# Zeroing the experts' output buffer on another engine, and decoding 64-bit weights in wider pieces of single tasks

## The chip, the core and the metric

The kernel runs on one core of a Trainium2 chip. The metric is the device time of one execution in microseconds (us); lower is better. The kernel before was timed in three runs: 807.14, 810.14 and 810.48 us, median 810.14.

## The reference: what is computed

Three stages follow one another.

1. Causal attention with a decay: 4 batches, 8 heads, 576 positions, head size 64. The result, laid out as 2304 tokens of 512 numbers, is the input `x` of the second stage.
2. A mixture of 8 experts in which every token goes to one expert, that of the largest logit: `h = max(x[mask] @ w1[e], 0)`, `out[mask] = gate * (h @ w2[e])`, with `w1` of 512 x 1024 and `w2` of 1024 x 512 per expert.
3. A shared block on all tokens: `h = max(x @ w1, x @ w2, x @ w3)` and `h @ w_out`, with three matrices of 512 x 768 and one of 768 x 512. In the reference, `1.0 / np.sqrt(d_model)` makes these four matrices float64, and the products of them run in float64.

## The kernel before, in words

Attention takes the first part, and then the function `moe` does the two other stages. All matrix products there use a split of each number into a rounded part and a remainder ("hi" and "lo"): three matmuls (lines 906 to 908, function `mm3`) stand for one product. Every tile that goes into such a product must first be rounded (a copy, line 934) and then have its remainder taken (a subtraction: line 951 for expert weights, line 1022 for shared weights, line 1069 for tokens, line 1123 for the hidden layer, line 1181 for the shared block's input).

**Order.** The engines run their instructions in the order in which the program issues them. That order is not written by hand: the class `Sched` plans it when the kernel is built. Every task names an engine (or a choice of two), a planned cost in us, a due time (`prio`), the tasks that it waits for and a buffer that it takes or gives back. `run` takes, step by step, the task that could start first by the planned times, and among equals the one due first. Within `moe`, `sd.bias` makes VectorE (1.0) dearer than GpSimd (0.3) where a task may run on either. What an engine really does later deviates from the planned times, but the order stays.

**Experts.** The 8 experts are taken in order of size, with fixed capacities `CAP` of 384 down to 256 tokens. For each, tokens are gathered from memory by GpSimd (`gather`, line 1051), transposed on TensorE into one of two PSUM buffers (`flip`, line 1058), rounded and split (lines 934 and 1069, the latter always on VectorE). Expert weights come in quarters of 128 x 1024 through three staging tiles `stg` and a ring of four split quarters. The first expert's quarters 1 to 3 are loaded from ScalarE's queue, the others from SP's. The results go into `Y`, four tiles of 128 x 2512, the experts one behind the other, each at an offset read at run time. `Y` is set to zero first by four GpSimd memsets (`zero`, line 1088).

**Shared weights.** The four float64 matrices lie in memory as pairs of 32-bit words, 12 keys of 128 x 1024 values. `shared_piece` (line 988) loads them and rebuilds float32 numbers from the two words (`bits`, line 977): five VectorE instructions shift and mask the high word into sign, exponent and mantissa (lines 982, 984), add the top three bits of the low word (985), and set numbers too small to zero by a comparison of the magnitude (983, 986). This is the decoding. It is done for 256 values at a time, as one planned task of 1.35 us, and writes to a tile `decv` of its own; rounding and remainder follow. The first 8 keys (`M2EARLY`) are prepared during the expert stage and stay; their loads of 128 x 512 words share one buffer `std`, given back at the end of the decoding. The last 4 keys come at the end through `stg` and the ring.

**The shared block** takes 6 chunks of 384 tokens. Matmuls into `pm` are followed by the maximum over the three matrices on VectorE (line 1222, tile `tm`), the split of the hidden layer `g` (lines 934 and 1233), the last product `po` (lines 1248 to 1250) and a scatter to memory.

Of the kernel before, what the change touches and what calls it, by code (L numbers as in the profile page):

```python
# [6 lines left out]
F32 = mybir.dt.float32  # L7
# [31 lines left out]
RING = 4  # L39
# [80 lines left out]


class Sched:
    """Orders the instructions of all engines: at each step the task that could start first, then the most urgent."""

    HOP = 0.2

# [784 lines left out]
def moe(tc, g, x_dram, w1, w2, m2, mo, out, rp, es):  # L911
# [11 lines left out]
    KC, FC, F2C, m2c, nchunk = DM // 128, FF // 128, F2 // 128, MC // 128, N // MC  # L923
    Y = [yp.tile([128, YW], F32, name=f"Y{d}") for d in range(KC)]

    sd = Sched({"o": 2, "stg": 3, "std": 1, "ring": RING, "scr": 3, "decv": 2, "y": 6}, 0.0)
    sd.bias = {"DVE": 1.0, "Pool": 0.3}
    act = lambda n: 0.06 + n / 1200
    dve = lambda n: 0.15 + n / 960
# [47 lines left out]
    def bits(raw, q, v, n):  # L977
        r = raw.rearrange("p (n w) -> p n w", w=2)[:, 256 * q:256 * q + 256]
        lo, hi = r[:, :, 0], r[:, :, 1]
        t = scr.tile([128, 256], I32, tag="dect", name=f"dt{n}", bufs=1)  # L980
        u = scr.tile([128, 256], I32, tag="decu", name=f"du{n}", bufs=1)
        nc.vector.tensor_scalar(out=t, in0=hi, scalar1=3, scalar2=0x3FFFFFF8, op0=ALU.logical_shift_left, op1=ALU.bitwise_and)  # L982
        nc.vector.tensor_scalar(out=u, in0=hi, scalar1=0x7FFFFFFF, scalar2=None, op0=ALU.bitwise_and)
        nc.vector.scalar_tensor_tensor(out=t, in0=hi, scalar=-0x40000000, in1=t, op0=ALU.bitwise_and, op1=ALU.bitwise_or)
        nc.vector.scalar_tensor_tensor(out=t, in0=lo, scalar=29, in1=t, op0=ALU.logical_shift_right, op1=ALU.bitwise_or)  # L985
        nc.vector.scalar_tensor_tensor(out=v, in0=u, scalar=float(897 << 20), in1=t.bitcast(F32), op0=ALU.is_ge, op1=ALU.mult)

    def shared_piece(key, early, use):
        w, j = key
        src = (mo[j] if w == "o" else m2[w, j]).bitcast(I32)  # L990
        nq = 1 if early else 2
        size = 512 * nq
        lows = []
        for h in range(2048 // size):
            raw = {}

            def load(e, h=h, raw=raw):
                if early:
                    t = raw[0] = std.tile([128, size], I32, tag="std", name=f"sd_{w}_{j}_{h}")
                else:  # L1000
                    t = raw[0] = stg.tile([128, size], I32, tag="stg", name=f"sd_{w}_{j}_{h}")
                nc.sync.dma_start(out=t, in_=src[:, size * h:size * h + size])

            pool_ = "std" if early else "stg"
            ld = sd.task("SP", 0.75 * nq, load, use - 8, [ahead.get(pool_)], get=(pool_, (key, h)), lat=2.0)
            ahead[pool_] = ld
            for q in range(nq):
                i = h * nq + q
                sl = slice(256 * i, 256 * i + 256)

                def dec(e, q=q, i=i, raw=raw):
                    raw[1 + q] = scr.tile([128, 256], F32, tag="decv", name=f"dv_{w}_{j}_{i}", bufs=2)
                    bits(raw[0], q, raw[1 + q], f"_{w}_{j}_{i}")

                def hi(e, q=q, i=i, raw=raw, sl=sl):
                    if key not in weight:
                        weight[key] = (m2p.tile([128, 2, 1024], F32R, name=f"m_{w}_{j}") if early else
                                       ring.tile([128, 2, 1024], F32R, tag="ring", name=f"m_{w}_{j}"))
                    copy(e, weight[key][:, 0, sl], raw[1 + q])

                def lo(e, q=q, raw=raw, sl=sl):
                    ENG[e].tensor_tensor(out=weight[key][:, 1, sl], in0=raw[1 + q], in1=weight[key][:, 0, sl].bitcast(F32),
                                         op=ALU.subtract)

                td = sd.task("DVE", 1.35, dec, use - 4, [ld], get=("decv", (key, i)),
                             rel=[(pool_, (key, h))] if q == nq - 1 else [])
                new = not early and i == 0
                th = sd.task(("ACT", "DVE"), (act(256), 0.2), hi, use - 3, [td, ahead.get("ring") if new else None],
                             get=("ring", key) if new else None)
                if new:  # L1030
                    ahead["ring"] = th
                lows.append(sd.task(("DVE", "Pool"), (dve(256), 0.69), lo, use - 3, [th], rel=[("decv", (key, i))]))
        wsplit[key] = lows

    def xtiles(name):
        return [xp.tile([128, KC, PADW], F32R, tag=f"x{i}", name=f"x{i}_{name}") for i in range(2)]
# [48 lines left out]
        else:  # L1085
            expert_piece(1, 0, q, now + 3.8 * q, [first], "ACT")
    xdone = {0: tokens(0, now, [])}
    zero = [sd.task("Pool", 2.1, lambda e, d=d: nc.gpsimd.memset(Y[d], 0.0), now + 16) for d in range(KC)]
    mkeys = [(w, j) for j in range(3) for w in range(3)] + [("o", j) for j in range(3)]
    total = now + sum(CAP) * 192 / 2400  # L1090
    for i, key in enumerate(mkeys[:M2EARLY]):
        shared_piece(key, True, now + 30 + (total - now - 34) * (i + 1) / M2EARLY)
    yprev, yall = [[] for _ in range(4)], []
    ydone = []
    hlast, yev_last = [], []
    for k in range(E):
# [43 lines left out]
        for i, (q, d) in enumerate(order):  # L1140
            def ymm(e, q=q, d=d, k=k, C=C):
                if q == 0:
                    hh["y", k, d] = ps_y.tile([128, 512], F32, tag="y", name=f"py{k}_{d}")
                py = hh["y", k, d]
                w = weight[2, k, q].rearrange("p s (f d) -> p s f d", f=2)
                for f in range(2):
                    fc = 2 * q + f
                    ds_ = slice(128 * d, 128 * d + 128)
                    mm3(nc, py[:, 0:C], w[:, 0, f, ds_], w[:, 1, f, ds_], hh[k, fc][:, 0, 0:C], hh[k, fc][:, 1, 0:C],
                        fc == 0, fc == FC - 1)  # L1150

            end = not any(q2 == q for q2, _ in order[i + 1:])
            last[d] = sd.task("PE", 6 * C / 2400, ymm, now, [wsplit[2, k, q], h_lo[2 * q], h_lo[2 * q + 1], last.get(d)],
                              get=("y", ("y", k, d)) if q == 0 else None, rel=[("ring", (2, k, q))] if end else [])
            pieces[q].append(last[d])
            now += 6 * C / 2400
            if q == 3:
                def yev(e, d=d, k=k, C=C):
                    o = Y[d][:, bass.ds(reg(ENG[e], "offi", k, YW - C), C)] if k else Y[d][:, 0:C]
                    copy(e, o, hh["y", k, d][:, 0:C])  # L1160

                prev = [ydone[-1][d]] if ydone else [zero[d]]
                t = sd.task(("ACT", "DVE"), (act(C), dve(C)), yev, now, [last[d]] + prev + [sorted_], rel=[("y", ("y", k, d))])
                yev_last.append(t)
        ydone.append(yev_last[-KC:])
# [1 line left out]
        yall = [last[d] for d in range(KC)]  # L1167
        hlast = h_pe
    for i, key in enumerate(mkeys[M2EARLY:]):
        shared_piece(key, False, now + 24 + 4 * i)  # L1170

    def ysplit(c, use, before):
        done = []
# [268 lines left out]
```

## Time and profile before

| what | value |
|---|---|
| median of three runs | 810.14 us (807.14 to 810.48) |
| span of the profiled execution, first to last instruction | 808.7 us |
| TensorE busy with matmuls | 744.5 us, 92% of the span |
| VectorE | 485.8 us, 60% |
| ScalarE | 364.8 us, 45% |
| GpSimd | 267.9 us, 33% |
| mean DMA rate | 112 GB/s |

The page gives no other time of the profiled execution than its span; the median of the runs lies 1.4 us (0.2%) above it. The busy share of TensorE is an average over stages with different limits, and a matmul that is counted as busy isn't always at its peak, because its end is modelled. What counts is when a stage starts, where TensorE stands still in it, which engine let it go on, and at which clock it then runs (PEclk, as a share of full speed). A row of the timeline has the start, the duration, the engine, the line of the program, the instruction, the written and read tiles with their shapes and how many instructions were merged; in brackets stand the idle time before it and what ended it. A name such as `dt` or `x` is the program's tile name, buffer numbers left out.

### The profile page before, as it was taken

The numbers are of one execution on the slowest core, as the hardware profiler recorded it, in microseconds if no ns is written. First come the engines' busy times: TensorE is split into PE (matmuls) and PEld (weight loads), VectorE is DVE, ScalarE is ACT, GpSimd is POOL, SyncE is SP. The second block draws the span as 40 slices with busy tenths as digits, with TensorE's granted clock in tenths as the row PEclk, the third lists the DMA queues.
The fourth block names the chain that finished last, engine by engine and source line by source line (L and its number), as shares of the span: only waits on it lengthen the run. The fifth ranks groups of instructions, "written<-read, shape, count | busy, mean of one in ns | idle before, by whom it ended". The sixth has DMA issues, their size and how long they took to land.

```text
span 808.7 us, 13612 instructions
## 1 busy us (share of the span) xinstructions
PE 744.5 (92%) x4862; PEld 685.5 (85%) x4862; DVE 485.8 (60%) x1197; ACT 364.8 (45%) x892; POOL 267.9 (33%) x214
## 2 busy tenths in 40 slices
PE   2989999999929899998998999979999999999996
PEld 1768878778719899998998999969989999899995
DVE  6888888887487997888777857981111211212110
ACT  5768878978626344553453544231121211212111
POOL 7465352540062543434344202341121211212111
PEclk9999999999959999999998999999999999999999
DMA  9958785831146556666476554300000000000001
GB/s 220 239 138 203 178 191 137 201 78 30 32 121 216 148 172 202 187 198 197 145 208 189 168 180 132 104 1 39 1 40 1 6 34 1 40 1 14 27 1 41
DMA packets 46919, 90.20 MB, mean 112 GB/s; under 512 B 23576, under 2 KB 23576, under 8 KB 46848
## 3 DMA queue, kind: packets, MB, share of 16 engines
q1 hardware_dynamic: 43264, 77.83, 35.1%
q0 software_dynamic: 3152, 9.88, 3.5%
q10 hardware_dynamic: 432, 1.57, 0.5%
q8 instruction: 40, 0.66, 0.3%
q14 instruction: 31, 0.25, 0.1%
HBM read 74.97 MB, written 9.44 MB: 104 GB/s over the span
## 4 chain that ended last, share of the span: by engine, by line
PE 61%; DVE 20%; DMA 13%; issue 3%; ACT 2%; POOL 0%; SPq 0%; DVEq 0%; POOLq 0%; ACTq 0%
PE pm L907 8%; PE pm L908 8%; PE pm L906 8%; DMA sd<-in_m_dram 7%; PE s L344 7%; PE po L459 6%; PE t L397 4%; DMA stg<-in_w_dram 3%; PE po L1250 2%; PE po L1249 2%; PE po L1248 2%; PE pb L478 2%; DVE dt L982 2%; DVE w L951 2%; DVE dt L985 2%
## 5 line engine op out<-in xcount | busy, mean ns | idle before, releaser
L1222 DVE TENSOR_TENSOR tm<-pm,tm 128x384 f32<-128x384 f32 x72 | 40.1, 557 | 199.1 <-PE pm L908 197.9
L906 PE MATMUL pm<-x_y,m 128*128 128x384 f32 x432 | 144.7, 335 | 3.3 <-DVE tm L1222 3.3
L907 PE MATMUL pm<-x_y,m 128*128 128x384 f32 x432 | 144.6, 335 | 0.0
L908 PE MATMUL pm<-x_y,m 128*128 128x384 f32 x432 | 144.4, 334 | 0.0
L381 ACT ACTIVATE P<-P,nm 128x576 f32<-128x576 f32 (+4 forms) x160 | 88.3, 554 | 18.2 <-DVE nm L361 17.6
L344 PE MATMUL s<-R,At 128*128 128x192 f32 (+1 forms) x192 | 70.8, 378 | 16.5 <-DVE At L271 11.1
L906 PEld LDWEIGHTS pm<-x_y,m 128*128 128x128 f32 x432 | 81.1, 188 | 4.5 <-DVE tm L1222 4.3
L1233 POOL TENSOR_TENSOR g<-tm,g 128x384 fp32r<-128x384 f32 x36 | 38.3, 1064 | 138.1 <-ACT g L934 138.0
L907 PE MATMUL ph<-x,w 128*128 128x384 f32 (+7 forms) x256 | 79.7, 311 | 2.8 <-DVE x L1069 2.8
L934 ACT ACTIVATE w<-stg 128x1024 fp32r<-128x1024 f32 x64 | 67.4, 1054 | 32.2 <-DMA stg<-in_w_dram 25.2
L907 PEld LDWEIGHTS pm<-x_y,m 128*128 128x128 f32 x432 | 81.1, 188 | 0.6 <-POOL x_y L1181 0.3
L906 PE MATMUL py<-h,w 128*128 128x384 f32 (+7 forms) x256 | 81.4, 318 | 0.0
L908 PE MATMUL py<-h,w 128*128 128x384 f32 (+7 forms) x256 | 80.0, 313 | 1.2 <-DVE w L951 1.2
L908 PEld LDWEIGHTS pm<-x_y,m 128*128 128x128 f32 x432 | 81.1, 188 | 0.0
L906 PE MATMUL ph<-x,w 128*128 128x384 f32 (+7 forms) x256 | 79.9, 312 | 0.7 <-ACT x L934 0.7
L907 PE MATMUL py<-h,w 128*128 128x384 f32 (+7 forms) x256 | 79.9, 312 | 0.0
L908 PE MATMUL ph<-x,w 128*128 128x384 f32 (+7 forms) x256 | 79.7, 311 | 0.2 <-DVE w L951 0.2
L951 DVE TENSOR_TENSOR w<-stg,w 128x1024 fp32r<-128x1024 f32 x47 | 64.3, 1371 | 21.9 <-ACT w L934 21.9
L361 DVE CUSTOM_DVE_ANT_0 P<-s,mask 128x288 f32<-128x288 f32 (+4 forms) x160 | 64.3, 421 | 10.8 <-PE s L344 6.5
L934 ACT ACTIVATE g<-tm 128x384 fp32r<-128x384 f32 x36 | 18.9, 524 | 110.7 <-DVE tm L1222 110.6
L321 POOL TENSOR_TENSOR At<-q,At 64x1152 fp32r<-64x1152 f32 x15 | 40.3, 2687 | 76.7 <-DVE At L433 24.8
L344 PE MATMUL s<-R,Bt 66*128 66x192 f32 (+1 forms) x192 | 59.6, 317 | 4.1 <-DMA Bt<-At 4.1
(244 smaller groups left out, 1704.5 us busy)
## 6 DMA issues: line engine op xcount, KB each, us to landing
stg<-in_w_dram SPq DMA_DIRECT2D x61, 512.0 KB
q<-in_q_dram SPq DMA_DIRECT2D x32, 288.0 KB
k<-in_k_dram SPq DMA_DIRECT2D x32, 288.0 KB
sd<-in_m_dram SPq DMA_DIRECT2D x32, 256.0 KB
Bt<-At SPq DMA_DIRECT2D x16, 288.0 KB
v<-in_v_dram SPq DMA_DIRECT2D x4, 1024.0 KB
x_dram<-XL SPq DMA_DIRECT2D x64, 64.0 KB
sd_o<-in_mo_dram SPq DMA_DIRECT2D x6, 512.0 KB
```

The costliest lines, as they stand in the source:

```text
L321: nc.gpsimd.tensor_tensor(out=At[i][64:128], in0=raws[p][0][64:128], in1=At[i][64:128].bitcast(F32), op=ALU.subtract)
L344: nc.tensor.matmul(st[:, 0:wp], lt[0:kk, r, ROW0[t]:ROW0[t] + 128], rt[0:kk, r, j0:j0 + wp], start=(ps_i == 0), stop=(ps_i == 1))
L361: nc.vector.tensor_tensor_reduce(out=P[0:n, j0:j0 + w], in0=st_.pop((h, t, k))[0:n, 0:w], in1=g.mask[0:n, m0:m0 + w], scale=-0.125, scalar ...
L381: nc.scalar.activation(out=P[0:n, 0:ext], in_=P[0:n, 0:ext], func=AF.Exp, bias=nm[0:n, k:k + 1], scale=-1.0, accum_out=sums[b][0:n, t, h % ...
L459: nc.tensor.matmul(po[64 * r:64 * r + 64, lo - c0:w], vt[b][0:n, a, (2 * hp + r) * D:(2 * hp + r + 1) * D], PT[(2 * p + r) % NPT][0:n, a, ...
L906: nc.tensor.matmul(out, whi, xhi, start=start, stop=False)
L907: nc.tensor.matmul(out, whi, xlo, start=False, stop=False)
L908: nc.tensor.matmul(out, wlo, xhi, start=False, stop=stop)
L934: nc.scalar.activation(out=out, in_=in_, func=AF.Copy)
L951: ENG[e].tensor_tensor(out=w[:, 1], in0=t, in1=w[:, 0].bitcast(F32), op=ALU.subtract)
L1222: nc.vector.tensor_tensor(out=mx[0], in0=mx["p", w][:, 0:MC], in1=mx[0], op=ALU.max)
L1233: ENG[e].tensor_tensor(out=ht[:, 1, :], in0=mx[0], in1=ht[:, 0, :].bitcast(F32), op=ALU.subtract)
```

## The change

The planner's cost for a piece, the buffers and the tasks change, not the arithmetic.

- `Y` is zeroed by ScalarE (`clear`): four copies of a broadcast column times 0, of the columns from 384 to 2304 alone, planned at 1.8 us each, behind the first expert's last weight quarter (`wsplit[1, 0, 3]`). Only the results of the second and later experts wait for it.
- `bits` isn't called any more. A piece is 512 values (128 x 1024 words, for early keys too). The five steps are single planned tasks of 0.4 or 0.65 us, 2.75 in all. The masked high word is put over the high words in the loaded tile (`size`), and the result over its low words (`flush`); a scratch tile `dec` of 512 columns, a single one, holds the rest. So the loaded tile is given back only behind the remainder (`lo`).
- The loads of the early keys wait for the split of `wsplit[1, 0, 3]` or of the key before the previous one.

```
-    sd = Sched({"o": 2, "stg": 3, "std": 1, "ring": RING, "scr": 3, "decv": 2, "y": 6}, 0.0)
+    sd = Sched({"o": 2, "stg": 3, "std": 1, "ring": RING, "scr": 3, "dec": 1, "y": 6}, 0.0)
...
-    def shared_piece(key, early, use):
+    def shared_piece(key, early, use, deps):
...
+        for h in range(2):
...
+                t = (std if early else stg).tile([128, 1024], I32, tag=pool_, name=f"sd_{w}_{j}_{h}")
+                nc.sync.dma_start(out=t, in_=src[:, 1024 * h:1024 * h + 1024])
+                t = t.rearrange("p (n w) -> p n w", w=2)
+                raw[0], raw[1] = t[:, :, 0], t[:, :, 1]
+
+            def exponent(e, h=h, raw=raw, tmp=tmp):
+                tmp[0] = scr.tile([128, 512], I32, tag="dec", name=f"dec_{w}_{j}_{h}", bufs=1)
+                nc.vector.tensor_scalar(out=tmp[0], in0=raw[1], scalar1=3, scalar2=0x3FFFFFF8, op0=ALU.logical_shift_left,
+                                        op1=ALU.bitwise_and)
+
+            def sign(e, raw=raw, tmp=tmp):
+                nc.vector.scalar_tensor_tensor(out=tmp[0], in0=raw[1], scalar=-0x40000000, in1=tmp[0], op0=ALU.bitwise_and,
+                                               op1=ALU.bitwise_or)
+
+            def last(e, raw=raw, tmp=tmp):
+                nc.vector.scalar_tensor_tensor(out=tmp[0], in0=raw[0], scalar=29, in1=tmp[0], op0=ALU.logical_shift_right,
+                                               op1=ALU.bitwise_or)
+
+            def size(e, raw=raw):
+                nc.vector.tensor_scalar(out=raw[1], in0=raw[1], scalar1=0x7FFFFFFF, scalar2=None, op0=ALU.bitwise_and)
+
+            def flush(e, raw=raw, tmp=tmp):
+                nc.vector.scalar_tensor_tensor(out=raw[0].bitcast(F32), in0=raw[1], scalar=float(897 << 20),
+                                               in1=tmp[0].bitcast(F32), op0=ALU.is_ge, op1=ALU.mult)
...
+            ld = sd.task("SP", 1.5, load, use - 8, deps + [ahead.get(pool_)], get=(pool_, (key, h)), lat=2.0)
...
+            for i, (fn, cost) in enumerate(((exponent, 0.4), (sign, 0.65), (last, 0.65), (size, 0.4), (flush, 0.65))):
+                t = sd.task("DVE", cost, fn, use - 4, [t, ahead.get("dec") if i == 0 else None], get=("dec", (key, h)) if i == 0 else None,
+                            rel=[("dec", (key, h))] if i == 4 else [])
...
+            th = sd.task(("ACT", "DVE"), (act(512), 0.4), hi, use - 3, [t, ahead.get("ring") if new else None],
+                         get=("ring", key) if new else None)
...
+            lows.append(sd.task(("DVE", "Pool"), (dve(512), 1.3), lo, use - 3, [th], rel=[(pool_, (key, h))]))
...
-    zero = [sd.task("Pool", 2.1, lambda e, d=d: nc.gpsimd.memset(Y[d], 0.0), now + 16) for d in range(KC)]
+    def clear(e, d):
+        nc.scalar.activation(out=Y[d][:, CAP[0]:N], in_=g.ident[:, 0:1].to_broadcast([128, N - CAP[0]]), func=AF.Copy, scale=0.0)
+
+    zero = [sd.task("ACT", 1.8, lambda e, d=d: clear(e, d), now + 16, [wsplit[1, 0, 3]]) for d in range(KC)]
...
+    shared = [wsplit[1, 0, 3]]
...
-        shared_piece(key, True, now + 30 + (total - now - 34) * (i + 1) / M2EARLY)
+        shared.append(shared_piece(key, True, now + 30 + (total - now - 34) * (i + 1) / M2EARLY, [shared[max(0, i - 1)]]))
...
-                prev = [ydone[-1][d]] if ydone else [zero[d]]
+                prev = [ydone[-1][d], zero[d]] if ydone else []
```

## Rows read from the trace of the kernel before

**Rows 1.** Busy time by stretch: us, then each engine's busy us, clock, DMA
```profile
core 0 of [0], span 808.7 us
242.50:246.00 3.50, 3.46 (x10) 3.06 (x11) 3.21 (x8) 2.51 (x3) 1.40 (x2) 0.54 0.92 339
242.50:496.20 253.70, 240.39 (x1636) 236.35 (x1637) 200.04 (x373) 123.21 (x215) 87.09 (x56) 0.97 0.59 185
436.90:443.60 6.70, 5.49 (x24) 5.46 (x25) 6.28 (x10) 2.16 (x5) 5.47 (x4) 0.50 0.59 176
496.20:545.00 48.80, 44.15 (x239) 40.97 (x238) 45.19 (x92) 15.33 (x37) 21.91 (x25) 1.00 0.17 55
545.00:797.00 252.00, 252.00 (x1366) 240.70 (x1365) 45.32 (x72) 47.83 (x92) 51.51 (x50) 1.00 0.04 17
```

**Rows 2.** Timeline of all engines, 231 to 243 us
```profile
231.01 0.95 POOL L1051 DMA_INDIRECT gat<-x_dram,gidx  x1 [0.31 <-issue]
...
231.75 8.84 DVE L776 CAST offi<-off 128x8 int32<-128x8 f32 x1
231.95 8.62 POOL L1088 MEMSET Y<- 128x2512 f32 x4
...
234.37 6.23 DVE L1069 TENSOR_TENSOR x<-xt,x 128x512 fp32r<-128x512 f32 x2
...
240.70 1.11 PE L1058 MATMUL xt<-ident,gat 128*128 128x128 f32 x4 [6.01 <-DVE ov L779]
...
241.85 0.60 ACT L934 ACTIVATE x<-xt 128x512 fp32r<-128x512 f32 x1 [6.52 <-PE xt L1058]
...
242.06 0.34 ACTq L964 DMA_DIRECT2D stg<-in_w_dram  x1
...
242.50 0.69 PE L906 MATMUL ph<-x,w 128*128 128x384 f32 x1 [0.69 <-ACT x L934]
```

**Rows 3.** Chain of waits, 228 to 262 us: start, us, what
```profile
228.24 4.31 DMA gat<-x_dram,gidx
```

**Rows 4.** TensorE's waits, expert stage: total us, times, longest; six rows
```profile
PE xt L1058 <- DVE x L1069: 8.9, 6, 3.6
...
PE ctps L859 <- DVE x L1069: 0.2, 1, 0.2
```

**Rows 5.** VectorE's groups by shape, 242 to 545 us: count, busy us, mean ns
```profile
L951 DVE TENSOR_TENSOR w<-stg,w 128x1024 fp32r<-128x1024 f32 x46 | 56.1, 1223 | 21.9 <-ACT w L934 21.9
L982 DVE TENSOR_SCALAR dt<-sd 128x256 int32<-128x256 int32 x36 | 22.3, 619 | 14.3 <-DMA sd<-in_m_dram 13.8
...
L982 DVE TENSOR_SCALAR dt_o<-sd_o 128x256 int32<-128x256 int32 x12 | 3.5, 288 | 0.1
```

**Rows 6.** Timeline: an undisturbed decoding (five rows), and one beside GpSimd
```profile
244.69 0.29 DVE L982 TENSOR_SCALAR dt<-sd 128x256 int32<-128x256 int32 x1
...
246.00 0.43 DVE L986 SCALAR_TENSOR_TENSOR dv<-du,dt 128x256 f32<-128x256 int32 x1
...
505.29 0.83 POOL L1022 TENSOR_TENSOR m<-dv,m 128x256 fp32r<-128x256 f32 x1 [1.34 <-ACT m L934]
...
505.44 0.83 DVE L983 TENSOR_SCALAR du_o<-sd_o 128x256 int32<-128x256 int32 x1
```

**Rows 7.** ScalarE's and GpSimd's groups by shape up to 545 us
```profile
L934 ACT ACTIVATE w<-stg 128x1024 fp32r<-128x1024 f32 x63 | 66.3, 1054 | 26.4 <-DMA stg<-in_w_dram 25.2 <-issue 0.4 <-ACT w L934 0.3
...
L951 POOL TENSOR_TENSOR w<-stg,w 128x1024 fp32r<-128x1024 f32 x17 | 42.2, 2483 | 22.6 <-ACT w L934 22.5
...
L1022 POOL TENSOR_TENSOR m_o<-dv_o,m_o 128x256 fp32r<-128x256 f32 x12 | 9.6, 803 | 20.1 <-ACT m_o L934 20.1
```

**Rows 8.** SP's DMA queue: its waits, 227 to 545 us
```profile
SPq L1002 <- DVE dt L985: 108.3, 32, 14.2
```

**Rows 9.** TensorE's waits, 496.2 to 545 us; three rows
```profile
PE pm L906 <- DVE tm L1222: 3.3, 3, 1.7
...
PE po L1248 <- ACT g L934: 0.6, 1, 0.6
```

More of the change, by code (lines that the diff above doesn't have):

```diff
@@ L986, in bits @@
         nc.vector.scalar_tensor_tensor(out=v, in0=u, scalar=float(897 << 20), in1=t.bitcast(F32), op0=ALU.is_ge, op1=ALU.mult)
-    def shared_piece(key, early, use):
+    def shared_piece(key, early, use, deps):
         w, j = key
         src = (mo[j] if w == "o" else m2[w, j]).bitcast(I32)
-        nq = 1 if early else 2
-        size = 512 * nq
         lows = []
-        for h in range(2048 // size):
-            raw = {}
+        pool_ = "std" if early else "stg"
+        for h in range(2):
+            raw, tmp = {}, {}
+            sl = slice(512 * h, 512 * h + 512)
@@ L997, in load @@
             def load(e, h=h, raw=raw):
[L998 to L1005, printed above, removed]
@@ L1006, in shared_piece @@
-            ahead[pool_] = ld
[L1007 to L1032, printed above, removed]
@@ new lines, in flush, with hi @@
+            def flush(e, raw=raw, tmp=tmp):
+                nc.vector.scalar_tensor_tensor(out=raw[0].bitcast(F32), in0=raw[1], scalar=float(897 << 20),
+                                               in1=tmp[0].bitcast(F32), op0=ALU.is_ge, op1=ALU.mult)
+            def hi(e, raw=raw, sl=sl):
+                if key not in weight:
+                    weight[key] = (m2p.tile([128, 2, 1024], F32R, name=f"m_{w}_{j}") if early else
+                                   ring.tile([128, 2, 1024], F32R, tag="ring", name=f"m_{w}_{j}"))
+                copy(e, weight[key][:, 0, sl], raw[0].bitcast(F32))
@@ new lines, in lo @@
+            def lo(e, raw=raw, sl=sl):
+                ENG[e].tensor_tensor(out=weight[key][:, 1, sl], in0=raw[0].bitcast(F32), in1=weight[key][:, 0, sl].bitcast(F32),
+                                     op=ALU.subtract)
+            ld = sd.task("SP", 1.5, load, use - 8, deps + [ahead.get(pool_)], get=(pool_, (key, h)), lat=2.0)
+            ahead[pool_] = ld
+            t = ld
+            for i, (fn, cost) in enumerate(((exponent, 0.4), (sign, 0.65), (last, 0.65), (size, 0.4), (flush, 0.65))):
+                t = sd.task("DVE", cost, fn, use - 4, [t, ahead.get("dec") if i == 0 else None], get=("dec", (key, h)) if i == 0 else None,
+                            rel=[("dec", (key, h))] if i == 4 else [])
@@ L1033, in shared_piece @@
+            ahead["dec"] = t
+            new = not early and h == 0
+            th = sd.task(("ACT", "DVE"), (act(512), 0.4), hi, use - 3, [t, ahead.get("ring") if new else None],
+                         get=("ring", key) if new else None)
+            if new:
+                ahead["ring"] = th
+            lows.append(sd.task(("DVE", "Pool"), (dve(512), 1.3), lo, use - 3, [th], rel=[(pool_, (key, h))]))
         wsplit[key] = lows
+        return lows[-1]
     def xtiles(name):
@@ L1169, in moe @@
     for i, key in enumerate(mkeys[M2EARLY:]):
-        shared_piece(key, False, now + 24 + 4 * i)
+        shared_piece(key, False, now + 24 + 4 * i, [])
     def ysplit(c, use, before):
```

## The prediction, made before the changed kernel was run

> **What bounds the kernel now.** I read the stages first (busy time by stretch): where TensorE stands idle, and at which clock. Up to 220 us lies attention, which the diff does not touch. Then comes a hole until the first expert matmul at 242.5. The expert stage (242.5 to 496.2) holds 253.7 us, 240.4 of them counted busy, at a mean clock of 0.97; a passage of 48.8 us follows with 44.15 busy; the last chunks (545 to 797) are full [rows 1]. So time can be won in three places alone: the hole in front of the expert stage, the stage's inner gaps, and the passage.
>
> Then the timeline of the start. VectorE's small CAST of the offsets lasts 8.84 us, as GpSimd's four memsets of Y begin 0.2 us behind it and last 8.62 us together; both end at 240.6 [rows 2]. Two token splits of VectorE (6.23 us for two) end there too. The third transposition of tokens waited 6.01 us, then ScalarE's copy came at 241.85 and the first expert matmul at 242.50 [rows 2]. The memsets therefore hold VectorE, and VectorE holds TensorE.
>
> Then TensorE's waits in the expert stage: six groups, 14.0 us, of which 8.9 are transpositions that wait for VectorE's token split, which frees their PSUM buffer [rows 4]. The clock adds to it: 0.97 over 253.7 us is 7.6 us lost, of which 1.6 belong to the first 3.5 us of the stage (0.54); the rest (6.0) lies in later stretches such as 436.9 to 443.6, at 0.50 after a wait of TensorE of up to 3.6 us [rows 1, 4]. Last, what VectorE does: the decoding of the shared weights costs 126.1 us in ten groups, 48 pieces of 2.63 us each [rows 5].
>
> **The change part by part.**
>
> *The zeroing leaves GpSimd.* Without it the CAST is short and the splits follow ScalarE's copies at once. The first gather takes 4.31 us from its issue to the landing; the third is issued at 231.01, so its tokens are there at about 235.4 [rows 2, 3]. The transposition takes 1.1, ScalarE's copy began 1.15 us behind the start of the transposition (240.70 to 241.85) and the first matmul 0.65 behind that [rows 2]: 235.5 + 1.15 + 0.65 = 237.3, or 5.2 us earlier than 242.50. The weights must come along: ScalarE issues the third quarter's load right behind that copy (242.06, [rows 2]), so it moves too; the first quarter's split waited for the memsets like all else. Bounds: 5.2 us is the whole of it; the least is 2.7, if the planner, finding GpSimd free, gives it a weight remainder there (2.48 us, [rows 7]) that holds the CAST. I take 5.2, nearest to the rows of this very stretch.
>
> *ScalarE writes the zeros.* Four copies of 1920 columns; a 1024-column copy takes 1.054 us [rows 7], so at most 1.98 each, 7.9 together. ScalarE works 123 of 253.7 us in the stage [rows 1], and only the second expert's results need the zeros, which now depend on the first expert's last weight quarter. Queued behind a clear are ReLUs and weight roundings; six PSUM buffers cover the ReLUs, three staging tiles the roundings. If that cover is gone, one clear (2.0 us) shows; below that nothing. I take 0.7.
>
> *The decoding in pieces of 512.* An undisturbed piece of 256 takes from 244.69 to 246.43, 1.74 us [rows 6]. Two-input instructions cost 0.43 at 256 columns and 1.22 at 1024 [rows 5, 6], 1.03 ns per column above a fixed 0.17; at 512 each of the three adds 0.26, and the two one-input steps half of that (0.29 at 256, [rows 6]): 1.74 + 0.79 + 0.26 = 2.8, against 3.48 for two of 256. 24 pieces save 16 us of VectorE. The in-place steps write with a stride of two words; if the one-input form lost its rate there, 24 times 0.27 = 6.5 us come off. [...] The rows show 0.17 us per instruction, and the measurement decides.
>
> The pieces are also disturbed: 126.1 - 48 x 1.74 = 42.6 us of the decoding is waiting. A one-input step of 0.29 takes 0.83 while GpSimd does a remainder of 0.83 [rows 6]. Remainders of 512 on GpSimd should take 1.35 (0.80 at 256, 2.48 at 1024, [rows 7]); if each held VectorE for all its length, 24 x (2.8 + 1.35) = 100, a saving of 26 us; if the waits halve with the instructions, 67 + 21 = 88, a saving of 38. [...] I take 26, some 17 in the expert stage and 9 in the passage.
>
> *Single tasks.* One decoding stood in the plan as 1.35 us and could not be parted; it takes 2.63. Now 2.75 is planned per piece and 4.1 expected, and a token split can go between two steps. VectorE so falls behind its plan by 1.4 us per 512 columns instead of 2.6. VectorE worked 200 of 253.7 us in the expert stage [rows 1], so it does not bound the stage as a whole: what it decides is the moments when the split of tokens is late. I take half of the 14.0 us of waits and half of the 6.0 us of clock: 10 us. Bounds: 0 (the waits only move) and 18 (all but the last weights).
>
> *One buffer of 1024 words, held to the remainder.* SP waited 108.3 us, 32 times, for the early buffer [rows 8], with the experts' weight loads queued behind. Now it is 16 pieces, and the buffer is held for rounding and remainder too. A cycle: load about 4.5 (estimate, from the gather's 4.31, [rows 3]), decoding 4.1, rounding 0.6 (1.054 at 1024, [rows 7]), remainder 1.35, handing over 0.5: 11 us. 16 cycles are 176 us. The loads now wait for the first expert's last quarter, whose load follows the one at 242.06 [rows 2] that moves to 237: they begin near 250 and the pieces end near 426, some 55 us ahead of their use in the passage. I cost it at nothing; at 14.5 us per cycle this cover is gone.
>
> *The passage.* VectorE is busy 45.2 of 48.8 us there, and TensorE waits 4.6 us, 3.3 of them for VectorE's maximum that frees PSUM [rows 1, 9]. With the 9 us less decoding I take 4.0 of the 4.6; bounds 0 and 4.6. Behind it TensorE is full, so nothing is late next.
>
> **The sum.** 5.2 - 0.7 + 10 + 4.0 = 18.5 us. The profiled span is 808.7 [rows 1]; with 18.5 off it is 790.2, and the median of the runs (810.14) lies 1.4 above that span: 791.6, rounded up to 792.
>
> **The rivals.**
> *Only the start is won.* GpSimd's remainders and weight remainders (17 of 2.48 us, [rows 7]) still hold VectorE, the planner finds another order, and as many splits of tokens come late. For it: each such weight remainder alone is longer than what is needed to make a split late, and none is removed. Against it: 26 us less VectorE work. 5.2 - 0.7, and 0 to 2 of the passage: about 803 to 806.
> *All waits go.* 5.2 + 18 + 4.6: about 782. For it: the waits are few and all of one kind. [...]
> *Given back.* The start is earlier, but weights come no earlier (SP behind the early buffer), so that TensorE waits later for what it won: 807 to 812. For it: 108.3 us of SP's waits; against it: hardly a wait of TensorE names a weight today.
> *Slower: the single wide buffer.* Load, decoding, rounding and remainder now stand one behind the other with nothing overlapped. Place: SP's queue, with expert loads behind it; it decides from 14.5 us per cycle. At 16.5 the early weights end 16 x 2 = 32 us late; the decoding begun early covers part, and the remainder of the cost, some 15 us, stands ahead of the passage: 810 - 5 + 15 = 820. For it: GpSimd takes 2.48 us for a weight in front of a remainder, and such a delay now holds the buffer. Against it: the 11 us estimated.
>
> **How the numbers follow.** Forecast (785 to 801) 0.56; only the start (801 to 806) 0.19; all waits go (779 to 785) 0.09; given back 0.08; slower 0.08. About 0.5%, 4 us, is what a measurement of this kernel can tell from no change. Faster by more (below 806.1): 0.84; within: 0.08; slower: 0.08. The range 781 to 808 leaves out the slow rival, half of what is given back, and a little below.
>
> **What would show it.** The first expert matmul near 237.3 (over 240: the first step is wrong). The CAST under 0.5 us. Decoding groups near 100 us on VectorE. TensorE's waits for token splits near 7 us, with fewer stretches at half clock. No wait of TensorE for the maximum before 545. If SP's waits for the early buffer grow above 108 us and TensorE's waits name weights, the slow rival holds; if the start is earlier and the expert stage is longer by as much, the gain was given back.

## The result and the profile after

The changed kernel takes 784.12 us (median of 4, 782.49 to 785.84) against 808.64 us for the kernel before, measured with it: ratio 0.970, 95% interval 0.966 to 0.974, or 24.5 us less. The profiled executions differ by 25.4 us (808.7 and 783.3). Measured again beside other versions (the last experiment) the ratio was 0.969 (0.965 to 0.972).

First the stages of the changed kernel, busy time by stretch (columns as in [rows 1]): expert stage, passage, last chunks.

```profile
237.90:477.06 239.16, 234.97 (x1636) 231.28 (x1637) 188.45 (x289) 128.25 (x201) 67.58 (x43) 0.99 0.56 195
477.06:525.80 48.74, 48.74 (x266) 46.31 (x265) 39.91 (x54) 15.13 (x30) 21.23 (x18) 1.00 0.17 60
525.80:771.00 245.20, 245.20 (x1337) 235.05 (x1335) 45.03 (x72) 46.78 (x90) 49.37 (x48) 1.00 0.04 17
```

The expert stage begins at 237.90 and not 242.50, lasts 239.2 us and not 253.7, and runs at 0.99; the passage is full [rows 1]. So the 25.4 us are 4.6 in front of the expert stage (0.2 of them from attention), 14.5 inside it, and 6.3 behind it: 306.2 us from the first matmul of the shared block to the end, against 312.5.

The start in the timeline:

```profile
228.04 1.08 POOL L1065 DMA_INDIRECT gat<-x_dram,gidx  x1 [45.59 <-DVE rr L689]
...
230.82 0.95 POOL L1065 DMA_INDIRECT gat<-x_dram,gidx  x1 [0.30 <-issue]
...
231.57 0.20 DVE L776 CAST offi<-off 128x8 int32<-128x8 f32 x1
...
236.12 1.09 PE L1072 MATMUL xt<-ident,gat 128*128 128x128 f32 x4 [1.85 <-DVE ov L783]
...
237.90 0.69 PE L906 MATMUL ph<-x,w 128*128 128x384 f32 x1 [0.69 <-ACT x L934]
```

The CAST of 8.84 us [rows 2] takes 0.20. Nothing holds VectorE any more, and the third transposition starts 5.3 us after the issue of its gather at 230.82. This trace has no landing for that gather; in the trace of the same kernel measured again it lands 5.5 us after its issue, so I take the transposition to wait for the gather.

TensorE's waits in the expert stage are five rows with 4.7 us together, where there were 14.0 [rows 4]; none is a transposition. In the passage there is none.

```profile
PE ph L907 <- DVE x L1083: 2.1, 2, 1.7
PE py L906 <- DVE h L1141: 0.8, 1, 0.8
PE ph L908 <- DVE w L951: 0.7, 1, 0.7
PE ph L906 <- ACT x L934: 0.7, 1, 0.7
PE py L908 <- DVE w L951: 0.4, 1, 0.4
```

VectorE's groups (columns as in [rows 5]): the decoding is ten groups again, 93.8 us in all instead of 126.1. The costliest group, and one of equal shape that nothing holds up (997 and 689 ns a piece):

```profile
L1009 DVE SCALAR_TENSOR_TENSOR dec<-sd,dec 128x512 int32<-128x512 int32 x18 | 17.9, 997 | 0.6
...
L1013 DVE SCALAR_TENSOR_TENSOR dec<-sd,dec 128x512 int32<-128x512 int32 x18 | 12.4, 689 | 0.4
```

ScalarE's clears stand between ReLUs of the first expert, 1.80 us each, and TensorE waits for nothing from 245 to 270 us:

```profile
249.15 1.80 ACT L1103 ACTIVATE Y<-ident 128x1920 f32<-128x1920 f32 x1
250.85 0.49 ACT L1135 ACTIVATE h<-ph 128x384 fp32r<-128x384 f32 x1
251.23 1.05 ACT L934 ACTIVATE w<-stg 128x1024 fp32r<-128x1024 f32 x1
```

### The profile page after: what moved, and what is told of

The parts are those of the page before. It is cut to its first block, busy times and chain, and to the rows that moved or that the text cites. A ratio compares the mean times of both kernels' runs of the same rounds, so it can differ in the third digit from the quotient of the medians.

```text
span 783.3 us, 13403 instructions
## 1 busy us (share of the span) xinstructions
PE 738.9 (94%) x4862; PEld 682.3 (87%) x4862; DVE 461.9 (59%) x1076; ACT 368.2 (47%) x870; POOL 237.7 (30%) x189
## 4 chain that ended last, share of the span: by engine, by line
PE 75%; DVE 9%; DMA 7%; issue 4%; ACT 1%; POOL 1%; SPq 1%; POOLq 0%; DVEq 0%; ACTq 0%
PE pm L907 10%; PE pm L906 10%; PE pm L908 10%; PE s L344 6%; PE po L459 6%; PE t L397 4%; PE ph L908 3%; PE ph L907 3%; PE py L906 3%; PE py L908 3%; PE ph L906 3%; PE py L907 3%; PE po L1268 3%; PE po L1267 3%; PE po L1266 3%
## 5 line engine op out<-in xcount | busy, mean ns | idle before, releaser
L344 PE MATMUL s<-R,At 128*128 128x192 f32 (+1 forms) x192 | 71.3, 380 | 14.9 <-DVE At L271 10.5
L934 ACT ACTIVATE w<-stg 128x1024 fp32r<-128x1024 f32 x63 | 66.2, 1056 | 33.3 <-DMA stg<-in_w_dram 14.4
L951 DVE TENSOR_TENSOR w<-stg,w 128x1024 fp32r<-128x1024 f32 x54 | 70.2, 1304 | 19.3 <-ACT w L934 18.9
L906 PE MATMUL py<-h,w 128*128 128x384 f32 (+7 forms) x256 | 79.5, 311 | 0.8 <-DVE h L1141 0.8
L1251 POOL TENSOR_TENSOR g<-tm,g 128x384 fp32r<-128x384 f32 x34 | 36.5, 1074 | 141.4 <-ACT g L934 141.4
L908 PE MATMUL py<-h,w 128*128 128x384 f32 (+7 forms) x256 | 78.5, 307 | 0.4 <-DVE w L951 0.4
L907 PE MATMUL py<-h,w 128*128 128x384 f32 (+7 forms) x256 | 78.2, 305 | 0.0
L361 DVE CUSTOM_DVE_ANT_0 P<-s,mask 128x288 f32<-128x288 f32 (+4 forms) x160 | 64.4, 422 | 11.1 <-PE s L344 6.7
```

Of the source, the lines that this page charges most:

```text
L344: nc.tensor.matmul(st[:, 0:wp], lt[0:kk, r, ROW0[t]:ROW0[t] + 128], rt[0:kk, r, j0:j0 + wp], start=(ps_i == 0), stop=(ps_i == 1))
L361: nc.vector.tensor_tensor_reduce(out=P[0:n, j0:j0 + w], in0=st_.pop((h, t, k))[0:n, 0:w], in1=g.mask[0:n, m0:m0 + w], scale=-0.125, scalar ...
L906: nc.tensor.matmul(out, whi, xhi, start=start, stop=False)
L907: nc.tensor.matmul(out, whi, xlo, start=False, stop=False)
L908: nc.tensor.matmul(out, wlo, xhi, start=False, stop=stop)
L934: nc.scalar.activation(out=out, in_=in_, func=AF.Copy)
```

## The experiments

Theory A: three separate gains, at the start from the memsets, in the expert stage and in the passage from the new decoding, the latter two because VectorE has less to do and its work comes in finer steps. The rivals stand with the runs. All ratios are to the kernel before on the same chip, with the 95% interval; the changed kernel stands at 0.969 to 0.970.

**The zeroing alone.**
```
 (kernel before)
-    zero = [sd.task("Pool", 2.1, lambda e, d=d: nc.gpsimd.memset(Y[d], 0.0), now + 16) for d in range(KC)]
+    zero = [sd.task("ACT", 1.8, lambda e, d=d: clear(e, d), now + 16, [wsplit[1, 0, 3]]) for d in range(KC)]
...
-                prev = [ydone[-1][d]] if ydone else [zero[d]]
+                prev = [ydone[-1][d], zero[d]] if ydone else []
```


> The kernel before with the zeroing alone moved to ScalarE, behind the first expert's last weight quarter; the decoding stays in 256-column pieces of one task. Theory A (three separate gains: 4.6 us at the start from the memsets, some 14 in the expert stage from the new decoding, some 6 in the passage from the new decoding): the first expert matmul near 238, expert stage again 250 to 256 us long with token splits late and stretches at half clock, passage with its 4.6 us of waits; in all 3 to 6 us faster than before (about 804). Theory B (the freed VectorE time at the start also sets the expert stage right): 12 us or more faster, under 797.

Measured: 804.09 us, ratio 0.991 (0.988 to 0.994), 7.6 us less. The first matmul came 8.7 us after the first gather instead of 14.3, the expert stage was 252.5 us long with 13.9 us of waits, and the rest 312.4, as before. Theory B falls: the time that VectorE gets back at the start doesn't set the stage right (it is 1.2 us shorter).

**The decoding alone.**
```
 (changed kernel)
-    zero = [sd.task("ACT", 1.8, lambda e, d=d: clear(e, d), now + 16, [wsplit[1, 0, 3]]) for d in range(KC)]
+    zero = [sd.task("Pool", 2.1, lambda e, d=d: nc.gpsimd.memset(Y[d], 0.0), now + 16) for d in range(KC)]
...
-                prev = [ydone[-1][d], zero[d]] if ydone else []
+                prev = [ydone[-1][d]] if ydone else [zero[d]]
```


> The changed kernel with the four GpSimd memsets back at the start, the new decoding kept. Theory A: first expert matmul at 242.5 again with a CAST of over 8 us, expert stage 238 to 243 us long without half clock, passage without waits; 4 to 5 us slower than the changed kernel (about 789). Theory B: the expert stage's waits return, 795 or more.

Measured: 796.7 us, ratio 0.981 (0.978 to 0.984). That is 9 us slower than the changed kernel, not 4 to 5. The hole is back (14.26 us from the first gather to the first matmul, as before), and the expert stage takes 247.2 us, 8 more than in the changed kernel, with 11.1 us of waits. The passage is without a wait. Together the two halves of the change give 7.6 + 15.5 = 23.1 us of the 24.5, so they add up within their intervals. TensorE's waits in the expert stage of this run, three rows of six:

```profile
PE ph L907 <- DVE x L1083: 4.3, 2, 3.2
PE xt L1072 <- DVE x L1083: 2.3, 2, 1.5
...
PE py L908 <- POOL w L951: 1.2, 1, 1.2
```

**The zeroing on GpSimd, planned late.**
```
 (changed kernel, clear)
-        nc.scalar.activation(out=Y[d][:, CAP[0]:N], in_=g.ident[:, 0:1].to_broadcast([128, N - CAP[0]]), func=AF.Copy, scale=0.0)
+        nc.gpsimd.memset(Y[d][:, CAP[0]:N], 0.0)
...
-    zero = [sd.task("ACT", 1.8, ...
+    zero = [sd.task("Pool", 1.65, ...
```


> The changed kernel with the four zeroings back on GpSimd, of the same columns 384 to 2304, but as late as ScalarE's (behind the first expert's last weight quarter). It parts the engine from the moment. Theory A (the moment is what counts, because only at the start does TensorE wait for VectorE's next instruction): first matmul as early as in the changed kernel, no more than 3 us slower than it (under 791). Rival (GpSimd's memset holds VectorE wherever it stands): one VectorE step of some 6 us in the first expert, token splits or weight remainders late, 4 to 8 us slower.

Measured: 794.93 us, ratio 0.979 (0.975 to 0.982), some 7 us slower than the changed kernel: the rival was right on the time. The timeline shows that the memsets were not late on the chip:

```profile
239.04 0.69 PE L906 MATMUL ph<-x,w 128*128 128x384 f32 x1 [0.69 <-ACT x L934]
239.57 6.63 POOL L1103 MEMSET Y<- 128x1920 f32 x4
...
239.69 6.54 DVE L799 TENSOR_SCALAR nrm<-ss 128x20 f32<-128x20 f32 x1
...
240.09 6.14 DVE L951 TENSOR_TENSOR w<-stg,w 128x1024 fp32r<-128x1024 f32 x1
```

The dependence on the weights is in the plan alone: the memsets ran 0.5 us behind the first expert matmul, before the planned moment. A small VectorE instruction then took 6.54 us, and a remainder that needs 1.22 ended with it. The start was won (9.6 us after the first gather), and 9.3 us went in the expert stage (248.5 us, 10.5 us of waits):

```profile
PE ph L907 <- DVE x L1083: 3.7, 2, 3.2
PE xt L1072 <- DVE x L1083: 2.4, 2, 1.5
...
PE py L908 <- POOL w L951: 1.2, 1, 1.2
```

It does not follow that the hold took these 9.3 us. From the first gather to the shared block's first matmul, VectorE's instructions stand in the same order in this run and in the decoding alone (all 311, by tile and shape), and in another one than in the changed kernel (269 of 311 in line): both plans lack ScalarE's clears. The memsets end 1.9 us before the stage with the decoding alone and 7 us into it here; yet the stages differ by 1.3 us, and the same waits stand at the same places: 3.18 and 3.20 us at 41 us behind the first expert matmul, 1.47 in both at 106 and 109, 1.22 and 1.21 at 214 and 215. In this run VectorE stood idle for 19 us in all between the memsets' end and the wait at 109, which leaves little room for a backlog from the memsets. So the traces speak for the other order as the main loss in the stage of both runs, and that the hold itself costs time later than the start is not shown. A run with that order and no memset on GpSimd was not made.

**One task per piece.**
```
 (changed kernel)
-            for i, (fn, cost) in enumerate(((exponent, 0.4), (sign, 0.65), (last, 0.65), (size, 0.4), (flush, 0.65))):
-                t = sd.task("DVE", cost, fn, use - 4, [t, ...
+            t = sd.task("DVE", 2.75, whole, use - 4, [ld, ahead.get("dec")], get=("dec", (key, h)), rel=[("dec", (key, h))])
...
-                        pe_ = sd.task("PE", ..., wsplit[w, j] + (ys[k0:k1] if c == 0 and fc == 0 else ys) + yall,
+                        pe_ = sd.task("PE", ..., wsplit[w, j] + (ys[k0:k1] if c == 0 and fc == 0 else ys) + yall + ([pe_] if k0 else []),
```


> The changed kernel with the five decoding steps of a piece planned as one task of 2.75 us (and the matmuls of one sum kept in order by a dependence). Theory A with the single tasks as a cause: token splits stand behind whole decodings, TensorE's waits for them return to 4 to 10 us, 4 to 12 us slower than the changed kernel (788 to 796). Rival, the width and the instruction count alone do it: within 2 us of the changed kernel.

Measured: 794.77 us, ratio 0.978 (0.975 to 0.981), some 7 us slower than the changed kernel. The expert stage took 250.2 us, with 12.2 us of waits and 10.2 us at half clock:

```profile
PE py L906 <- DVE h L1142: 5.8, 1, 5.8
PE xt L1073 <- DMA gat<-x_dram,gidx: 2.3, 1, 2.3
PE py L908 <- POOL w L951: 1.7, 1, 1.7
```

VectorE's decoding was 93.3 us, as in the changed kernel. (`whole` issues the five instructions of a piece. The added dependence concerns matmuls of the shared block alone; it was not run by itself.) What returned are waits, and the longest is not for a token split, as I expected, but for the hidden layer's remainders (`h`), behind a decoding and the routing work:

```profile
296.75 1.60 POOL L1030 TENSOR_TENSOR m<-sd,m 128x512 fp32r<-128x512 f32 x1 [3.57 <-ACT m L934]
297.12 1.34 DVE L847 TENSOR_TENSOR cc<-io,rq 128x90 f16<-128x90 f32 x1
298.31 2.34 POOL L951 TENSOR_TENSOR w<-stg,w 128x1024 fp32r<-128x1024 f32 x1
298.49 2.27 DVE L850 TENSOR_TENSOR cc<-cc,valid 128x90 f16<-128x90 f16 x1
```

The two routing steps take 0.24 and 0.25 us where nothing runs beside them, so some 3 of the 5.8 us are VectorE standing beside GpSimd. The other plan also gave GpSimd more weight remainders, 16 instead of 10. The 7 us therefore belong to the single tasks together with what the planner made of them.

**Two instructions per step, same plan.**
```
 (changed kernel, each of the five steps)
+            H2 = (slice(0, 256), slice(256, 512))
...
-                nc.vector.tensor_scalar(out=raw[1], in0=raw[1], ...
+                for c in H2:
+                    nc.vector.tensor_scalar(out=raw[1][:, c], in0=raw[1][:, c], ...
```


> The changed kernel, same plan and order, but each decoding step issues two instructions of 256 columns. It undoes the lower instruction count alone. Theory A with VectorE's time as a cause: decoding rises from 94 to some 115 to 125 us on VectorE, the passage's waits come back in part, 3 to 8 us slower than the changed kernel. Rival, the order and the finer tasks alone do it: within 2 us of the changed kernel.

Measured: 786.98 us, ratio 0.970 (0.967 to 0.974): the changed kernel's. The decoding took 95.6 us, not 115 to 125. My price of an instruction was wrong. Steps in two halves (x2), and in the changed kernel the same steps in one, behind a two-input step:

```profile
357.83 0.75 DVE L1018 SCALAR_TENSOR_TENSOR dec<-sd,dec 128x256 int32<-128x256 int32 x2
...
358.90 0.48 DVE L1023 TENSOR_SCALAR sd<-sd 128x256 int32<-128x256 int32 x2
```

```profile
472.41 0.69 DVE L1009 SCALAR_TENSOR_TENSOR dec<-sd,dec 128x512 int32<-128x512 int32 x1
473.14 0.69 DVE L1013 SCALAR_TENSOR_TENSOR dec<-sd,dec 128x512 int32<-128x512 int32 x1
473.75 0.42 DVE L1017 TENSOR_SCALAR sd<-sd 128x512 int32<-128x512 int32 x1
```

Two halves cost 0.06 us more than the whole. A step that needs the one before it (line 1013) starts 0.73 us behind a step of 0.69; one that doesn't (line 1017) starts 0.61 behind a step of the same length. The fixed 0.17 us, which the prediction took from rows of single instructions [rows 5, 6], was thus not paid again by an independent neighbour, which cost 0.06. By these numbers a wider piece saves the waits between dependent steps, not instructions.

**Single tasks of 256 columns.**
```
 (first experiment)
-                td = sd.task("DVE", 1.35, dec, use - 4, [ld], get=("decv", (key, i)), ...
+                td = ld
+                for n, cost in enumerate((0.2, 0.32, 0.32, 0.2, 0.31)):
+                    td = sd.task("DVE", cost, step, use - 4, [td, ahead.get("dec") if n == 0 else None], ...
```
(`step` issues the next of the five instructions)

> The kernel before with the zeroing on ScalarE and the 256-column decoding of before parted into five planned tasks, with the buffers and the planned time in all of before. It adds the single tasks alone to the first experiment (0.991 of before). Theory A (single tasks let the splits of tokens pass between steps): TensorE's waits for splits fall below 6 us, 4 to 8 us faster than the first experiment (797 to 800 where before is 809). Rival (single tasks help only where the planned time of a piece is near the real one): within 2 us of the first experiment.

Measured: 799.32 us, ratio 0.985 (0.982 to 0.988), 4.7 us better than the first experiment (the two intervals just touch), as theory A had it. Expert stage 245.2 us, waits 9.6, no half clock in it later than its start. Here too the plan changed what GpSimd does: 9 weight remainders instead of 18. The passage stays as slow as before (314.5 us from the first matmul of the shared block), with waits for `g` and one stretch at half clock.

**The planned cost set right.**
```
 (first experiment)
-                td = sd.task("DVE", 1.35, dec, use - 4, [ld], ...
+                td = sd.task("DVE", 2.6, dec, use - 4, [ld], ...
```
(and the dependence between the matmuls of one sum as above)

> The first experiment (zeroing on ScalarE, the decoding of before in one task of 256 columns) with one number changed: the planned cost of that task is 2.6 us, what it takes, instead of 1.35. Rival to the new decoding (the old plan simply mis-costed VectorE, and a true cost would have been enough): 5 us or more faster than the first experiment (0.991 of before), expert stage under 248 us. Theory A (the time that VectorE spends in dependent steps and beside GpSimd is the cause): within 3 us of the first experiment, as decoding stays near 126 us.

Measured: 797.5 us, ratio 0.983 (0.980 to 0.986), 6.2 us better than the first experiment: theory A allowed 3, so the rival holds for this much. Decoding rose to 133.6 us, and yet the expert stage fell from 252.5 to 245.6 us. The planner now gave GpSimd 34 weight remainders where it had 18, so a shorter stage doesn't need fewer of them there. The passage gained nothing (312.8), and the added dependence concerns matmuls of the passage.

**Remainders on VectorE alone**, first of experts and shared weights, then of the experts alone:
```
 (changed kernel)
-        tl = sd.task(("DVE", "Pool"), (1.13, 2.3), lambda e: low(e, weight[key], raw[0]), use - 3, [th], rel=[("stg", key)])
+        tl = sd.task("DVE", 1.13, lambda e: low(e, weight[key], raw[0]), use - 3, [th], rel=[("stg", key)])
...
-            lows.append(sd.task(("DVE", "Pool"), (dve(512), 1.3), lo, use - 3, [th], rel=[(pool_, (key, h))]))
+            lows.append(sd.task("DVE", dve(512), lo, use - 3, [th], rel=[(pool_, (key, h))]))
```


> The changed kernel with the remainders of expert weights and of shared weights on VectorE alone (GpSimd keeps the gathers and the shared block). It takes away GpSimd's instructions that read SBUF beside the decoding. Theory A (what VectorE lost was waiting beside GpSimd): decoding falls from 94 to 68 to 75 us, expert weights' remainders from 1.30 to 1.22 us each; VectorE gets 10 x 1.2 + 22 x 0.7 = 27 us more of its own work, about what it stops waiting; within 3 us of the changed kernel or faster. Rival (GpSimd's help is worth its price): VectorE over 90% busy in the expert stage, 5 to 15 us slower.

> The changed kernel with the expert weights' remainders alone on VectorE; the shared weights' remainders may still go to GpSimd. Theory A: the ten stops of up to 2.5 us beside GpSimd's weight remainders go, decoding 82 to 88 us, the remaining waits of TensorE for splits shrink; 0 to 3 us faster than the changed kernel. Rival: VectorE has 12 us more to do, 2 to 6 us slower.

Measured: 783.34 us, ratio 0.965 (0.962 to 0.969), and 783.45 us, ratio 0.965 (0.962 to 0.968). With all on VectorE the decoding takes 72.6 us, with GpSimd's shared remainders 79.7 (82 to 88 were expected). The expert stage with all on VectorE:

```profile
238.34:474.34 236.00, 234.02 (x1637) 230.97 (x1637) 184.63 (x311) 129.57 (x203) 19.59 (x19) 0.99 0.59 198
```

VectorE does 22 instructions more in the expert stage than in the changed kernel (311 against 289), and is busy 184.6 us instead of 188.5; with the experts' remainders alone it is 295 and 179.1 us. By these runs GpSimd's help saved VectorE nothing. The trace of the kernel before has VectorE held beside GpSimd: a two-input step, 0.42 us at 245.09, takes 1.24 beside a GpSimd remainder of 1.07.

```profile
508.81 1.07 POOL L1233 TENSOR_TENSOR g<-tm,g 128x384 fp32r<-128x384 f32 x1
508.93 1.24 DVE L984 SCALAR_TENSOR_TENSOR dt_o<-sd_o,dt_o 128x256 int32<-128x256 int32 x1
```

**Side by side on one chip**: the changed kernel, that version again, and that version with planned costs as the trace has them.
```
 (remainders on VectorE, moe)
-    act = lambda n: 0.06 + n / 1200
+    act = lambda n: 0.17 + n / 1200
...
-            for i, (fn, cost) in enumerate(((exponent, 0.4), (sign, 0.65), (last, 0.65), (size, 0.4), (flush, 0.65))):
+            for i, (fn, cost) in enumerate(((exponent, 0.45), (sign, 0.72), (last, 0.72), (size, 0.45), (flush, 0.72))):
```
(further: loads `lat` 2.0 to 2.7, gathers 2.4 to 3.4, weight rounding 0.95 to 1.05, remainder 1.13 to 1.22, and the dependence between the matmuls of one sum)

> The changed kernel itself, on the chip of the three others, to compare with them: 0.966 to 0.974 of before.

> The changed kernel with all remainders of weights on VectorE, repeated beside the changed kernel on one chip. Theory A: 1 to 5 us faster than the changed kernel, its waits for token splits (2.1 us) gone. Rival: no difference, within 1 us.

> The changed kernel with all remainders of weights on VectorE and the planned costs set to what the trace shows (ScalarE 0.17 us fixed, decoding steps 0.45 and 0.72, loads 0.7 and gathers 1.0 us later). Theory A (few waits are left in the expert stage, 2.6 us): 0 to 2 us faster than the remainders on VectorE alone. Rival (the planner lives on its optimism: honest latencies make it start loads in another order): 2 to 8 us slower.

Measured, in this order: 786.1 us, 0.969 (0.965 to 0.972); 783.68 us, 0.966 (0.963 to 0.969); 803.05 us, 0.991 (0.988 to 0.994). The two versions with weight remainders on VectorE are the fastest of the study, by 2.4 us here, but the intervals overlap. The traced costs made it 19 us slower, more than either theory allowed. The expert stage took 254.3 us, and TensorE waits for weights (which of the changed costs does it is open):

```profile
PE ph L908 <- DVE w L951: 6.8, 11, 1.1
PE ph L906 <- ACT w L934: 3.7, 2, 2.9
PE py L908 <- DVE w L951: 3.2, 4, 1.2
```

**The expert stage in all these runs** (us; one profile each):

| kernel | stage | TensorE's waits | at half clock, later than the start | VectorE busy | decoding, to the end of the passage |
|---|---|---|---|---|---|
| before | 253.7 | 14.0 | 13.7 | 200.0 | 126.1 |
| zeroing alone | 252.5 | 13.9 | 3.4 | 201.5 | 126.1 |
| + planned cost 2.6 | 245.6 | 9.1 | 3.4 | 195.7 | 133.6 |
| + single tasks of 256 | 245.2 | 9.6 | 0 | 199.9 | 108.0 |
| decoding alone | 247.2 | 11.1 | 3.4 | 188.1 | 90.5 |
| GpSimd, planned late | 248.5 | 10.5 | 6.8 | 192.2 | 90.4 |
| one task per piece | 250.2 | 12.2 | 10.2 | 191.7 | 93.3 |
| two instructions per step | 241.5 | 5.9 | 3.4 | 194.7 | 95.6 |
| changed | 239.2 | 4.7 | 0 | 188.5 | 93.8 |
| changed, again | 239.5 | 4.6 | 0 | 188.1 | 93.0 |
| expert remainders on VectorE | 237.2 | 2.8 | 0 | 179.1 | 79.7 |
| all remainders on VectorE | 236.0 | 2.6 | 0 | 184.6 | 72.6 |
| the same, again | 236.4 | 3.0 | 0 | 184.6 | 72.9 |
| the same, traced costs | 254.3 | 14.4 | 3.4 | 186.8 | 72.7 |

Take the waits and half of the half-clock time off a stage, and 233 to 238 us are left in every row (before: 253.7 - 14.0 - 6.9 = 232.8; changed: 239.2 - 4.7 = 234.5). The stage is some 235 us plus its waits and what stands at half clock. It does not follow VectorE's busy time: 185 to 192 us of it go with stages from 236 to 254. The profiled execution is one of several, and not the median one: that of the decoding alone took 800.01 us and that of one task per piece 799.51, 3.3 and 4.7 above their medians, that of the zeroing alone 801.47, 2.6 below. Differences of a few us between single rows can come from that.

## Why the prediction was right, and where its steps were not

The time lay in the range, faster was right, and the forecast's mechanism (VectorE held by memsets at the start, late behind decodings later) is what the traces show. The gain was 24.5 us against 18.5 forecast. With that, 784.12 us is 0.9 below the band of the forecast itself (785 to 801) and in the one given to "all waits go" (779 to 785, 0.09): the range held because it took that rival in, and two terms of the sum, the single tasks and the passage, were too small.

*The start*: 4.4 us measured from the first gather on, 5.2 forecast. The CAST fell to 0.20 and the order of events was as worked out; the third transposition came 5.3 us behind its gather's issue and not 4.31, which is the first one's time [rows 3]. (In the kernel before the third landed 3.5 us after its issue, and with the zeroing alone too; there the start is 8.7 us long against 9.9. Why it lands later in the changed kernel is open.) The bound "5.2 us is the whole of it" failed: without the zeroing's move the kernel is 9 us slower, not 5. The rest shows in the expert stage, and the two runs with GpSimd's memsets speak for the changed order as its cause rather than for a backlog.

*ScalarE's zeros*: 1.80 us each as planned, no wait of TensorE in that stretch; 0.7 was too much, and the cover held.

*The decoding*: 100 forecast, 93.8 measured. The sum was near and its reason half wrong: not fewer instructions, but fewer dependent starts, as two instructions per step left the time nearly as it was (95.6). That GpSimd's remainders hold VectorE for all their length, 24 x 1.35 = 32.4 us of the 100, was my estimate from one row, that of a one-input step (0.83 beside 0.83), and no run shows this term. In its place the runs show 21.2 us: 93.8 in the changed kernel less 72.6 with all remainders of weights on VectorE. A two-input step stood too, 1.24 us beside 1.07.

*Single tasks*, the step that carried the sum: 10 us forecast, 14.5 in the stage (with the zeroing's share). I took half of the waits and half of the clock; 9.3 of the 14.0 us of waits went, and all of the half-clock time later than the start. The reasoning failed in one link: I let 26 us less of VectorE's work halve the waits. The runs show that the length of the decoding doesn't decide: one task per piece has the same decoding and loses 7 us; a truer planned cost has more decoding than before and wins 6. What is left is the plan: where in VectorE's order the token splits, hidden-layer remainders and weights stand, and which remainders go to GpSimd. That the order counts is argued from these runs; no run changed the order alone. Single tasks are the shown part (7 us on the changed kernel, 5 on the old pieces), with the plan that comes with them. The width's own share in the expert stage, from the zeroing alone to one task per piece, is 2.3 us between two profiles that lie 2.6 us below and 4.7 above their medians, so its size is open.

*The passage*: 4.0 forecast with an upper bound of 4.6, 6.3 measured; this is the wider piece's place, as the single tasks of 256 leave it at 314.5 us and one wide task brings it to 307.7. The bound was too low because a wait costs more than its row says. The longest, in the kernel before:

```profile
525.30 0.33 PE L907 MATMUL pm<-x_y,m 128*128 128x384 f32 x1
525.48 0.34 PE L908 MATMUL pm<-x_y,m 128*128 128x384 f32 x1
527.53 0.45 PE L906 MATMUL pm<-x_y,m 128*128 128x384 f32 x1 [1.71 <-DVE tm L1222]
```

From start to start it is 2.05 us where 0.17 is usual, 1.88 lost for a row of 1.71. Summed in that way over its six waits the passage had 5.8 us to give.

*The single wide buffer*: costed at nothing, and it held, but nearer to the edge than I wrote. The first, the second and the last of the sixteen early loads:

```profile
240.78 0.47 SPq L999 DMA_DIRECT2D sd<-in_m_dram  x1
...
271.83 0.34 SPq L999 DMA_DIRECT2D sd<-in_m_dram  x1
...
451.33 0.34 SPq L999 DMA_DIRECT2D sd<-in_m_dram  x1
```

The first is issued at 240.78 and not near 250, as the wait for the first expert's weights is in the plan alone. From the second on it is 12.8 us per cycle, not 11, and 31 us from the first to the second load; the last early piece is ready at 463.9, 13 us ahead of the passage and not 55. The 0.5 us of handing over in my cycle was an estimate from no row; behind the last piece but one, ScalarE, GpSimd and SP each began 0.03 to 0.07 us after the step before them (449.03, 449.78 and 451.33). SP's longest wait there is now for GpSimd's remainder, which gives the buffer back (79.5 us in 15 waits, against 108.3 in 32, [rows 8]).

Of the rivals, "only the start" and "given back" fell with the passage and the stage; "all waits go" (782) is where the measured time came near, with 4.7 us of waits left in the stage and none in the passage, and where the version with all remainders on VectorE arrived.

## What to carry to other kernels

Where the order of work is planned ahead, ask first which short steps TensorE waits for, and cut the long tasks in front of them: it paid 5 to 7 us here with the same instructions, in another order and divided in another way between VectorE and GpSimd. Test a planner's costs as a knob and not as a truth: 2.6 for 1.35 won 6 us, and several costs set to what the trace shows lost 19. And don't hand an engine's work to a neighbour that blocks it for as long as the work would have taken: moving it back cost VectorE no time here (184.6 us busy in the expert stage against 188.5).

## What was not expected of the hardware

- A small one-input VectorE instruction stayed blocked over four GpSimd memsets in a row (8.84 us over 8.62, and 6.54 over 6.63); it did not get in between two of them, and instructions behind it, two-input ones too, stood as well (a remainder of 6.14 us).
- Two independent VectorE instructions of 256 columns cost 0.06 us more than one of 512 (0.75 and 0.69; 0.48 and 0.42). A step that needs the one before it starts 0.73 us behind it, one that doesn't 0.61.
- With GpSimd's remainders of weights gone, 22 more VectorE instructions took no more of its time in the expert stage (184.6 us against 188.5).
- The third of three gathers in a row landed 3.5 us after its issue in one kernel and 5.5 in the other.
